# Re-planning units 0 to 3 of a hand-ordered attention and mixer kernel

## The chip, the cores and the metric

The kernel runs on one core of a Trainium2 chip. The metric is device time in microseconds (us) of one launch, here the median of several runs. The core has a matrix engine (TensorE, PE in the profile), three elementwise engines (VectorE is DVE, ScalarE is ACT, GpSimd is POOL), a queue that only issues transfers (SyncE, SP) and 16 DMA engines that the queues share. Each engine works through its own list of instructions in order; semaphores join them.

## The reference

Pooled attention, eight batches of eight heads, followed by an MLP mixer whose weights are `w_tok1`, `w_tok2`, `w_ch1` and `w_ch2`:

```python
# q, k, v: (8, 8, 576, 64); pool = 8; scale = 1 / sqrt(64)
k_p = k.reshape(B, H, Sp, pool, D).mean(axis=3)          # 72 pooled keys
v_p = v.reshape(B, H, Sp, pool, D).mean(axis=3)
scores = scale * np.matmul(q, k_p.transpose(0, 1, 3, 2))
attn = softmax(scores)                                    # written out in the original
x = np.matmul(attn, v_p) as (B, S, H * D)                 # (8, 576, 512)

h = np.maximum(x.transpose(0, 2, 1) @ w_tok1, 0.0) @ w_tok2   # 576 -> 256 -> 576
u = x + h.transpose(0, 2, 1)
h2 = np.maximum(u @ w_ch1, 0.0) @ w_ch2                       # 512 -> 1536 -> 512
return u + h2
```

## The kernel before, in words

**Units.** The last part of a batch, the channel MLP, is a *unit*: a Python generator (`unit_fast`) that issues a few matmuls and yields. Units 0 to 7 are the batches' first 512 rows, unit 8 holds the remaining 64 rows of all batches. A plain unit, which 0 to 3 are, has 45 yields, called steps 0 to 44. Steps 0 to 23 are the first layer: 12 tiles (`l1_tile`, L526) of four 128x512 matmuls, two to a step, each tile emptied from PSUM by ScalarE with a Relu into a part of `GT` (L530). Steps 24 to 44 are the second layer, made of seven products of 12 matmuls 128x256 each (L674), three steps to a product: x (24 to 26), y (27 to 29), z (30 to 32), x again (33 to 35), w (36 to 38), z again (39 to 41), x again (42 to 44). Behind each product VectorE adds the bank to what is kept so far (L717). The products are of a Strassen kind: seven stand for eight, and their operands are sums.

**Sums.** `g_sums` makes four sums of quarters of `GT`: `=3` from the first six tiles (wanted by the last x product, step 42), `=1` (by z, step 30), `=2` from `=1` (by the second x product, step 33) and `=4` from `=2` (by the second z product, step 39). `=` puts a sum on VectorE, `+` on GpSimd. `weight_sum`, written w0 to w3, makes four sums of `w_ch2` once, in unit 0, on VectorE. All work on two bf16 operands in SBUF, 128x1536. In the profile the operand tiles are called `area`, the lines are L554 and L569.

**The plan.** While a unit runs, other batches' steps are woven in. `PLAN[n]` says for unit n behind which yield which steps are issued, in the order of the text. `HEAD` is a list of the same kind for what comes before unit 0. `b.name` is a step of batch b:

- `lk`, `lv`, `lq`: loads of keys, values and queries, issued by GpSimd (L121, L131). Two buffers each (`kr`, `vr`, `qb`).
- `K0`, `K1`, `V0`, `V1`: pooling of half the heads on GpSimd (`pool8`: L177, L178 and L181 or L183); `k0`, `v1` the same on VectorE. `kpool`, `vpool0`, `vpool1`: pooling on TensorE (L256, L267).
- `kpT`: pooled keys transposed (L225), copied by ScalarE (L227). `Q0`, `Q1`: queries transposed on VectorE (L287). `s0`, `s1`, `s2`: scores (L300) and their exponentials on ScalarE (L309); s0 takes Q0, s1 takes Q1, s2 both.
- `av0` to `av4`: attention times values (L388), with the division by VectorE (L392, L331); `aw` is the same with the multiplication on ScalarE, as eight instructions (L335). Scores and these products use two large PSUM buffers in turn (`p` in the profile).
- `at0`, `at1`: the first token matmul (L400, Relu L402). `u0` to `u4`: the second (L422, L417) and the residual, added by VectorE (L423). `t0` to `t3`: u transposed by TensorE (L431) and copied by ScalarE (L432).
- `M0`, `M2`, `M4`, `M`, `MT`: u is written to memory by SyncE and read back in another order (L441, L453), and `T0` to `T5` transpose it on VectorE (L465); this takes the place of `t` from batch 3 on.
- `g`: a gate. VectorE writes one element (L840) and GpSimd copies it (L841), so what is behind it on GpSimd waits until VectorE has come there; the next gate's write waits for the copy before.

**What sets the order.** Each engine's list is the order of the text, restricted to that engine. So a step's place matters for an engine only against that engine's other instructions, and a DMA issue on GpSimd stands behind GpSimd's sums and gates. TensorE works on four small PSUM banks (`p1a` to `p1d`) which `take` and `give` hand round first in, first out: whoever takes a bank waits until the one before has been emptied.

Of the kernel before, what the change touches and what calls it, by code (L numbers as in the profile page):

```python
# [17 lines left out]
SYNC = mybir.EngineType.SP  # L18


HEAD = """LkA LkT LkB LvT Lq LvA LvB Lt1 Lk1 Lt2 Lc1b Lc1a Lq1 Lc1c Lv1 Lc1d p1 Lc2a Lc2b Lc2c d2 d2 d3 d1 d4 d4 c0 c1 prep q0 kp0 kp1 kt0 q1 d1 o0 kt1 kp2 e0 e1 q3 kt2 o1 q2 e3 vpool0 o3 e2 a00 vpool1 a02 o2 m01 d1 d1 m00 a04 X1 m03 a14 m02 X0 m04 p0 a10 a12 1.kpool m10 m14 m12 m13 m11 A1 A0 X2 X3 A2 A3"""
PLAN = [
# [13 lines left out]
def kernel(  # L36
# [829 lines left out]
    with tc.manual_schedule(engines={PE, POOLE, DVE, ACT, SYNC}):  # L866
# [8 lines left out]
        for i in range(2):  # L875
            nc.vector.memset(values[i][:, :, D], float(POOL))
            nc.vector.memset(exps[i][:, H * S:], 0.0)
            nc.vector.memset(rests[i], 0.0)
        for i, s in enumerate(HEAD.split()):
            if i == 3:  # L880
# [34 lines left out]
```

## Time and profile before

| | |
|---|---|
| median of 3 runs | 263.99 us (263.57 to 265.01) |
| time of the profiled execution | 262.58 us |
| its span, first to last instruction | 260.8 us |
| granted TensorE clock | 1.0 |
| TensorE busy | 253.0 us (97%), 2172 matmuls |
| VectorE busy | 194.9 us (75%), 391 instructions |
| GpSimd busy | 159.0 us (61%), 168 |
| ScalarE busy | 125.4 us (48%), 229 |
| GpSimd waiting at gates for VectorE | 48.4 us, 24 times |

In the profile a row of the timeline has start, duration (us), engine, line, operation, output<-inputs, shape and count, and in brackets the idle time before it with what ended it. Matmuls overlap in the pipe: one of 128x512 shows 379 ns alone and starts 0.217 us after the one before, so TensorE's pauses are read from start to start. A stage's row has, for each engine, busy time and number of instructions.

### The profile page before, as it was taken

How to read it: one execution, taken by the hardware profiler on the slowest of the kernel's cores; microseconds unless marked ns; L12 is line 12 of the kernel's file. 1: busy time of each engine (PE TensorE's matmuls, PEld its weight loads, DVE VectorE, ACT ScalarE, POOL GpSimd, SP SyncE). 2: the span in 40 equal slices, each digit the busy share in tenths (PEclk: the TensorE clock that was granted, in tenths of full speed). 3: DMA queues.
4: the chain of work that ended last, by engine and by line, in shares of the span. 5: the costliest groups of instructions: out<-in, count | busy, mean ns of one | idle time of the engine just before them, and what ended most of it. 6: DMA issues, size and time to landing. Idle time of an engine off the chain costs nothing.

```text
span 260.8 us, 5503 instructions
## 1 busy us (share of the span) xinstructions
PE 253.0 (97%) x2172; PEld 167.8 (64%) x2193; DVE 194.9 (75%) x391; ACT 125.4 (48%) x229; POOL 159.0 (61%) x168
## 2 busy tenths in 40 slices
PE   8999999999999999999999999999999999999994
PEld 3785465764666644774487447754784478888883
DVE  3557559996689756977899548954695389999993
ACT  2354876049836555565750476065525421723610
POOL 8666326899989999588939971898307912100000
PEclk9999999999999999999999999999999999999999
DMA  7999999993091989599744942840405052602304
GB/s 154 192 201 207 205 206 210 205 208 95 3 153 30 130 212 213 122 152 249 165 123 66 205 160 77 136 118 1 147 21 159 16 155 61 176 0 61 102 4 161
DMA packets 31706, 34.31 MB, mean 132 GB/s; under 512 B 3136, under 2 KB 23744, under 8 KB 31680
## 3 DMA queue, kind: packets, MB, share of 16 engines
q0 software_dynamic: 17632, 17.64, 42.5%
q1 hardware_dynamic: 13632, 15.93, 20.5%
q10 hardware_dynamic: 416, 0.39, 0.5%
q8 instruction: 17, 0.28, 0.5%
q14 instruction: 9, 0.07, 0.1%
HBM read 38.99 MB, written 12.58 MB: 198 GB/s over the span
## 4 chain that ended last, share of the span: by engine, by line
PE 89%; DVE 5%; DMA 2%; issue 2%; ACT 0%; POOL 0%; DVEq 0%; ACTq 0%; POOLq 0%
PE p1a L674 8%; PE p1c L526 8%; PE p1d L674 7%; PE p1a L526 7%; PE p1b L674 7%; PE p1b L526 7%; PE p1d L526 6%; PE p1c L674 5%; PE p L388 4%; PE p L300 3%; PE p L647 2%; DMA kr<-in_k_dram 2%; PE p1d L400 2%; PE p1b L400 2%; PE p1c L422 2%
## 5 line engine op out<-in xcount | busy, mean ns | idle before, releaser
L526 PEld LDWEIGHTS <-w_ch 128*128 128x128 bf16 x336 | 30.2, 98 | 34.0 <-issue 3.0
L674 PEld LDWEIGHTS <-area 128*128 128x128 bf16 x432 | 41.3, 98 | 7.9 <-issue 1.0
L841 POOL COPY flag<-flag 1x1 f32<-1x1 f32 x35 | 10.2, 292 | 48.5 <-DVE flag L840 48.4
L309 ACT ACTIVATE ex<-p 72x768 bf16<-72x768 f32 x42 | 31.6, 803 | 16.3 <-PE p L300 16.3
L674 PEld LDWEIGHTS <-GT 128*128 128x128 bf16 x312 | 29.6, 98 | 7.0 <-issue 1.8
L178 POOL TENSOR_TENSOR t<-t 72x512 f32<-72x512 f32 x22 | 30.6, 1389 | 1.7
L526 PE MATMUL p1c<-uT,w_ch 128*128 128x512 bf16 x89 | 24.6, 379 | 0.2
L177 POOL TENSOR_TENSOR t<-vr 72x1024 f32<-72x1024 bf16 x11 | 23.5, 2136 | 1.3 <-DMA vr<-in_v_dram 0.7
L177 POOL TENSOR_TENSOR t<-kr 72x1024 f32<-72x1024 bf16 x11 | 23.9, 2177 | 0.4
L526 PE MATMUL p1a<-uT,w_ch 128*128 128x512 bf16 x82 | 22.3, 380 | 0.2
L526 PE MATMUL p1d<-uT,w_ch 128*128 128x512 bf16 x76 | 21.6, 379 | 0.2
L526 PE MATMUL p1b<-uT,w_ch 128*128 128x512 bf16 x77 | 21.2, 379 | 0.2
L331 DVE TENSOR_TENSOR x<-p,den 128x512 bf16<-128x512 f32 x28 | 19.4, 691 | 1.0
L530 ACT ACTIVATE GT<-p1a 128x512 bf16<-128x512 f32 x21 | 12.6, 602 | 14.8 <-PE p1a L526 7.4
L530 ACT ACTIVATE GT<-p1c 128x512 bf16<-128x512 f32 x23 | 13.9, 604 | 8.3 <-PE p1c L526 8.3
L554 DVE TENSOR_TENSOR area<-GT 128x1536 bf16<-128x1536 bf16 x9 | 12.2, 1355 | 5.6 <-ACT AT L402 5.1
L530 ACT ACTIVATE GT<-p1b 128x512 bf16<-128x512 f32 x20 | 12.0, 600 | 9.1 <-PE p1b L526 5.5
L388 PEld LDWEIGHTS <-ex 72*128 72x128 bf16 x280 | 12.8, 98 | 5.3 <-DVE xt L331 0.7
L530 ACT ACTIVATE GT<-p1d 128x512 bf16<-128x512 f32 x20 | 12.0, 601 | 7.2 <-PE p1d L526 6.4
L121 POOL DMA_DIRECT2D kr<-in_k_dram x17 | 10.9, 645 | 6.5 <-PE p1c L526 2.1
L388 PE MATMUL p<-vp,ex 72*128 72x65 bf16 x280 | 14.0, 194 | 0.2 <-DVE xt L331 0.2
L423 DVE TENSOR_TENSOR u<-p1c,x 128x512 bf16<-128x512 f32 x11 | 8.0, 729 | 7.9 <-PE p1c L422 6.0
(240 smaller groups left out, 546.6 us busy)
## 6 DMA issues: line engine op xcount, KB each, us to landing
out_dram<-o SPq DMA_DIRECT2D x32, 256.0 KB, 3.8
qb<-in_q_dram POOLq DMA_DIRECT2D x7, 576.0 KB, 10.5
kr<-in_k_dram POOLq DMA_DIRECT2D x7, 512.0 KB, 9.2
vr<-in_v_dram POOLq DMA_DIRECT2D x7, 512.0 KB, 14.5
w_ch<-in_moe_w_ch_dram POOLq DMA_DIRECT2D x5, 512.0 KB, 14.7
mem<-u SPq DMA_DIRECT2D x10, 256.0 KB, 2.1
v<-mem SPq DMA_DIRECT2D x20, 128.0 KB, 2.9
area<-in_q_dram SPq DMA_DIRECT2D x2, 288.0 KB, 3.0
```

Source lines behind the costliest of these rows:

```text
L121: nc.gpsimd.dma_start(out=t[j0:j1, h0:h1].rearrange("j h i d -> j h (i d)"), in_=src[b, h0:h1].rearrange("h (j i) d -> j h (i d)", i=POOL) ...
L177: eng.tensor_tensor(out=t4[:, 0:n], in0=t[:, hs, 0:4], in1=t[:, hs, 4:8], op=ALU.add)
L178: eng.tensor_tensor(out=t4[:, 0:n, 0:2], in0=t4[:, 0:n, 0:2], in1=t4[:, 0:n, 2:4], op=ALU.add)
L309: nc.scalar.activation(out=dst, in_=src, func=AF.Exp, scale=scale)
L331: nc.vector.tensor_tensor(out=dst, in0=view, in1=den[:, :, :, None].broadcast_to([n, a, 4, D]), op=ALU.mult)
L388: nc.tensor.matmul(out=ps[:, h // 4, (h % 4) * (D + 1):(h % 4 + 1) * (D + 1)], lhsT=st["ex"][:, h * S + n0:h * S + n0 + P], rhs=st["vp"][: ...
L400: nc.tensor.matmul(out=ps, lhsT=w_tok1[:, c if c < 4 else 4 + par, m * P:(m + 1) * P], rhs=st["x"][:, c, :] if c < 4 else st["xt"], start= ...
L526: nc.tensor.matmul(out=ps, lhsT=w_ch1[:, kk, m * P:(m + 1) * P], rhs=uT[kk], start=(kk == 0), stop=(kk == 3))
L530: nc.scalar.activation(out=GT[:, :, m, :], in_=ps.rearrange("p (h n) -> p h n", h=2), func=AF.Relu)
L554: eng.tensor_tensor(out=out, in0=a, in1=b, op=ALU.subtract)
L674: nc.tensor.matmul(out=ps[i] if split else ps[:, i], lhsT=chunk(u, i, a(m)), rhs=w(m), start=start and m == 0 and (i == 0 or split), stop= ...
L841: nc.gpsimd.tensor_copy(out=flag[:, 1:2], in_=flag[:, 0:1])
```

## The change

Nothing but the two tables changes: `HEAD` gets three steps at its end that stood in unit 0, and rows 0 to 3 of `PLAN` are new. Units 4 to 8 and all functions stay. The same matmuls are issued. Besides the order:

- `3.av0` (unit 1, step 43) becomes `3.aw0`: the multiplication goes from VectorE to ScalarE.
- `=4` of unit 3 becomes `+4`: the sum goes from VectorE to GpSimd.
- Gates: unit 0 has four in place of five, at other places (17, 17, 18 and 23, the last ahead of `=1`; before 13, 18, 23, 26 and 43). Unit 1 has 3, 25, 26 and 38 (before 18, 25, 28, 38); unit 2 has 14, 20, 32, 39, 41 (before 12, 32, 38, 40); unit 3 has 34 (before 28).
- Loads: in unit 0 `2.lq` goes from step 3 to 13, `2.lv` from 8 to 19 (behind three gates), `3.lk` now comes ahead of `3.lv`. `4.lq` goes from step 11 of unit 1 to 21, `5.lk` from unit 1 to the start of unit 2, `6.lv` from the end of unit 2 to step 9 of unit 3.

```diff
--- before.py
+++ after.py
@@ -18,12 +18,12 @@
 SYNC = mybir.EngineType.SP
 
 
-HEAD = """LkA LkT LkB LvT Lq LvA LvB Lt1 Lk1 Lt2 Lc1b Lc1a Lq1 Lc1c Lv1 Lc1d p1 Lc2a Lc2b Lc2c d2 d2 d3 d1 d4 d4 c0 c1 prep q0 kp0 kp1 kt0 q1 d1 o0 kt1 kp2 e0 e1 q3 kt2 o1 q2 e3 vpool0 o3 e2 a00 vpool1 a02 o2 m01 d1 d1 m00 a04 X1 m03 a14 m02 X0 m04 p0 a10 a12 1.kpool m10 m14 m12 m13 m11 A1 A0 X2 X3 A2 A3"""
+HEAD = """LkA LkT LkB LvT Lq LvA LvB Lt1 Lk1 Lt2 Lc1b Lc1a Lq1 Lc1c Lv1 Lc1d p1 Lc2a Lc2b Lc2c d2 d2 d3 d1 d4 d4 c0 c1 prep q0 kp0 kp1 kt0 q1 d1 o0 kt1 kp2 e0 e1 q3 kt2 o1 q2 e3 vpool0 o3 e2 a00 vpool1 a02 o2 m01 d1 d1 m00 a04 X1 m03 a14 m02 X0 m04 p0 a10 a12 1.kpool m10 m14 m12 m13 m11 A1 A0 X2 X3 A2 A3 0.u1 0.u3 1.kpT"""
 PLAN = [
-    {0: "0.u0 2.lk 0.u1 1.Q0 1.Q1", 2: "1.kpT", 3: "3.lq 2.lq", 5: "0.u3", 6: "1.s0", 7: "0.u2", 8: "2.lv", 9: "1.s1", 11: "1.vpool1", 12: "1.s2 1.vpool0", 13: "=3 g", 14: "1.av2", 15: "1.av1", 17: "1.aw0", 18: "1.av4 g", 19: "w0", 20: "3.lv 1.av3", 22: "w1", 23: "g =1 =2 3.lk", 25: "1.at1 1.at0 =4", 26: "g 2.K1", 27: "2.K0", 28: "w3", 29: "2.V0", 33: "1.u0", 34: "1.u1", 35: "1.u2", 36: "w2", 37: "2.Q1 1.t2", 40: "1.u3", 41: "1.t0", 42: "1.t3", 43: "g 1.t1 3.Q0 2.Q0 1.u4"},
-    {0: "2.kpT", 1: "2.v1", 3: "2.s0", 8: "3.K1 2.s2", 9: "3.K0", 11: "4.lq", 12: "2.s1", 15: "3.Q1", 16: "2.aw3", 17: "2.av1", 18: "g", 20: "2.av0", 21: "2.av4", 23: "2.av2 =1", 24: "4.lk", 25: "g", 26: "3.kpT 2.at1", 27: "=2", 28: "2.at0 =4 g", 31: "2.u3 4.Q1", 32: "3.s2", 33: "2.t3 2.u2", 35: "3.s0 3.V1", 36: "=3", 37: "3.V0", 38: "g 2.u1", 39: "4.lv 3.s1 2.u0", 40: "5.lk", 41: "4.Q0 2.t2 2.t0", 43: "2.t1 3.av0 3.av2"},
-    {4: "4.K1", 6: "3.av3 3.av4", 9: "3.av1 4.K0", 12: "g 3.at1", 13: "6.lk", 14: "=3 3.at0", 18: "4.kpT 4.V1", 19: "3.u1 4.V0", 20: "3.u0 3.u3", 21: "3.u2 3.u4", 23: "4.s2", 24: "3.M0 3.M2", 25: "=1", 26: "3.M4", 27: "=2", 28: "4.s0", 29: "=4", 30: "3.M", 31: "4.s1 3.MT 3.T3 3.T0", 32: "g 5.lq 5.lv", 34: "3.T1", 35: "4.av4 4.aw1", 36: "3.T2", 38: "g 6.lq", 40: "g", 42: "4.aw2 6.lv"},
-    {1: "4.av0", 3: "5.K1", 5: "4.av3", 8: "4.at1", 9: "4.at0 5.k0", 10: "5.Q0", 11: "4.u2", 12: "5.V0", 13: "4.u1", 15: "5.kpT 4.u3 5.V1", 16: "4.M2", 17: "5.s0", 18: "=3 5.Q1", 19: "6.Q0", 22: "4.u0", 23: "5.s1", 24: "4.M0", 25: "3.T4 =1 3.T5", 26: "=2", 27: "=4", 28: "g", 29: "4.M", 30: "5.s2", 32: "5.av0", 35: "5.av2", 37: "5.av1", 40: "5.av3 5.av4", 42: "4.T3 4.T1 4.T0", 43: "4.T2 5.at0 5.at1"},
+    {0: "1.Q1", 1: "2.lk 0.u0", 3: "1.Q0 3.lq", 6: "1.s0 0.u2", 9: "1.s1 1.vpool0", 10: "1.vpool1", 12: "=3 1.s2", 13: "2.lq", 14: "1.av2", 15: "1.av1", 17: "g 1.av4 g", 18: "g", 19: "1.aw0 2.lv w0", 20: "3.lk 1.av3", 22: "3.lv", 23: "w1 g =1 =2 =4", 24: "1.at0", 25: "1.at1", 28: "w3", 29: "1.u1", 33: "1.u2 1.u0", 34: "2.K1", 35: "2.K0", 36: "2.V0", 37: "1.t2 w2", 39: "1.u3", 41: "1.t0", 42: "1.t3", 43: "1.t1 3.Q0 2.Q0 1.u4", 44: "2.Q1"},
+    {0: "3.K0 2.kpT", 2: "2.s0", 3: "g", 7: "2.s2", 9: "2.v1", 12: "2.s1", 16: "2.aw3", 17: "2.av1", 20: "2.av0", 21: "3.K1 2.av4 4.lq", 23: "2.av2 =3", 24: "4.lk =1", 25: "g", 26: "g =2 2.at1", 27: "3.kpT", 28: "2.at0 3.s0", 30: "2.u3 3.Q1", 31: "3.V1", 32: "2.u2", 33: "2.t3 =4", 35: "4.Q1 2.t2", 37: "3.V0", 38: "3.s2 4.lv g", 39: "2.u0", 40: "2.u1 3.s1", 41: "2.t1 2.t0", 42: "4.Q0", 43: "3.aw0 3.av2"},
+    {0: "5.lk", 1: "4.K1", 3: "3.av1", 4: "3.av4", 6: "3.av3", 9: "4.K0", 10: "6.lk", 11: "3.at0", 13: "=3", 14: "g 3.at1", 19: "3.u2 4.V0 4.kpT", 20: "3.u0 4.V1 3.u1 3.u3 g", 21: "3.M0 3.M2", 22: "3.u4", 24: "3.M4 4.s2", 27: "=1 =2", 28: "4.s0", 30: "=4 3.M", 31: "4.s1 3.MT", 32: "3.T0 3.T3 g 5.lq", 33: "5.lv", 34: "4.aw1", 35: "6.lq 4.av4", 39: "g 3.T1", 40: "3.T2", 41: "g 4.aw2"},
+    {1: "4.av0", 5: "4.av3", 9: "4.at1 4.at0 6.lv 5.k0 5.K1", 11: "4.u2 4.u1", 13: "3.T5 5.V0", 14: "5.V1 5.Q0", 15: "5.kpT 4.u3", 17: "6.Q0 5.s0 5.Q1", 19: "=3 4.M2", 22: "3.T4 4.u0", 24: "5.s1", 25: "4.M0 =1", 26: "=2", 27: "+4", 30: "5.s2", 33: "5.av2 5.av0", 34: "g", 37: "4.M 5.av1", 38: "4.T3", 39: "4.T1 5.av3", 40: "5.av4", 42: "4.T0", 43: "4.T2", 44: "5.at1 5.at0"},
     {2: "6.K1", 5: "7.lq 7.lk 5.u3", 6: "5.u2", 8: "5.u0", 10: "6.K0", 11: "6.kpT", 12: "5.u1 6.V1 6.V0", 13: "5.M0", 16: "6.s0", 17: "5.M2", 18: "5.M", 20: "7.Q1", 21: "7.Q0", 22: "6.Q1 g", 23: "=1", 24: "6.s1 =3", 26: "g", 28: "=2", 29: "6.s2 5.T1", 30: "g", 32: "g 7.lv 5.T3", 34: "5.T0 =4", 36: "g", 37: "g", 41: "5.T2", 42: "6.av3", 44: "6.av0 5.u4"},
     {0: "7.K0", 2: "6.av2", 6: "6.av1", 7: "6.av4", 8: "7.K1", 9: "6.at0 7.V1 g", 10: "7.kpT g", 12: "=3", 13: "6.at1 g", 14: "g", 17: "6.u3 7.V0", 18: "6.u1", 20: "g 6.u2 7.s0", 21: "6.u0", 24: "7.s1", 25: "=1", 27: "=2 6.M2", 32: "7.av1", 33: "6.M0 =4", 35: "6.M", 36: "7.s2", 37: "g", 39: "6.T0 6.T2", 40: "g", 41: "6.T3", 42: "6.T1", 44: "7.av2 g 7.av3"},
     {1: "Z0", 4: "7.av0", 6: "7.av4", 8: "7.at1", 10: "Z1", 15: "7.at0", 16: "Z2", 17: "7.u1 7.u0 7.M0 7.u3 7.u4", 19: "7.u2", 20: "=3 Z3", 22: "7.M2", 25: "g =1", 27: "=2 7.M", 28: "g", 33: "=4", 34: "g", 35: "g 7.T3", 37: "7.T1 7.M4 7.T2", 38: "7.T0", 42: "7.y0", 43: "g 7.y1", 44: "7.Y2"},
```

## The prediction

> **What bounds the kernel now.** I read the busy times by stage first, then TensorE's instructions in order of time, then VectorE and GpSimd side by side where TensorE paused. The stages are cut near the starts of units 0 to 4 (first L526 matmuls at 24.25, 56.68, 86.82, 114.54 and 143.97 us).
>
> ```profile
> core 0: us, PE busy (x) PEld busy (x) DVE busy (x) ACT busy (x) POOL busy (x), PEclk, DMA share, GB/s
> 26.30:56.80 30.50, 29.94 (x259) 18.97 (x261) 23.71 (x43) 16.48 (x33) 18.05 (x20) 1.00 1.21 205
> 56.80:84.50 27.70, 27.18 (x254) 16.16 (x257) 21.60 (x34) 19.04 (x37) 25.72 (x24) 1.00 0.43 83
> 84.50:113.00 28.50, 28.40 (x257) 17.61 (x257) 21.28 (x38) 15.53 (x30) 24.44 (x24) 1.00 0.78 160
> 113.00:141.00 28.00, 27.89 (x256) 17.66 (x256) 23.80 (x44) 14.98 (x33) 22.23 (x21) 1.00 0.72 157
> ```
>
> TensorE (first pair of columns) fills every stage that the change touches, at full granted clock; VectorE and GpSimd sit at 75 to 90%. A busy share is not work, so I added up start-to-start times: 0.217 us for a 128x512 matmul, 0.109 for a 128x256, 0.26 for eight of L388, 0.47 for a scores group of L300. Beyond these prices, from 24 to 144 us, TensorE loses time in four places only, three of which carry these marks:
>
> ```profile
> 40.04 0.43 PE L388 MATMUL p<-vp,ex 72*128 72x65 bf16 x8 [0.17 <-DVE xt L331]
> 50.41 1.03 PE L674 MATMUL p1c<-area,GT 128*128 128x256 bf16 x8
> 51.63 0.40 PE L431 MATMUL p1d<-ident,u 128*128 128x128 bf16 x4 [0.18 <-DVE u L423]
> 83.02 0.59 PE L422 MATMUL p1b<-AT,w_tok 128*128 128x512 bf16 x2 [0.25 <-DVE flag L840]
> ```
>
> 0.34 us before 40.04 (the pair before it began at 39.27 and needs 0.43), 0.47 between 49.86 and 51.63 (0.43 + 8 x 0.109 = 1.30 of 1.77), 0.32 before 83.02, 0.24 inside the scores group at 107.37: 1.37 us. From 144 to 230 us I find none. Each time TensorE waits for VectorE to empty a bank, or for ScalarE's exponentials.
>
> **The ceiling.** The new plan issues the same matmuls. So units 0 to 3 can give back 1.37 us at most, 0.5% of 263.99. What decides is whether the new order makes waits of its own.
>
> **Head.** 0.u1, 0.u3 and 1.kpT come 1 to 5 steps earlier. They need banks emptied by A1, A0 and A2 (VectorE's last copy 24.02 + 0.69 = 24.71; kpT arrives at 24.25 + 0.86 = 25.11). Unit 0's first tile then takes A3's bank, emptied by ScalarE at 24.45 + 0.59 = 25.04, and arrives at 25.24. VectorE does u1, u3, 1.Q1, u0, 1.Q0 by about 28.4 (three adds of 0.73, two transposes of 0.71 behind 24.71, with small gaps); 1.s0 wants 1.Q0 at about 28.7. Cost 0, with 0.1 to 0.3 us to spare; without it 0.2.
>
> **vpool0 and vpool1** move up 3 and 1 steps, to about 31.6 us. Batch 1's values land at 16.50 + 14.6 = 31.1 and 19.15 + 12.2 = 31.35. Cost 0 to 0.2; I take 0.
>
> **Loads.** On GpSimd 2.lq moves only among steps that make it wait for nothing new. 2.lv falls behind three gates, so its issue goes from 34.31 to about 40. The DMA engines are full until 58 us (205 GB/s) and loads land in the order of issue: 2.lq still lands at 49.6 and 2.lv behind it at about 52.3, as before. 3.lk and 3.lv change places, both wanted after 60 us. Cost 0.
>
> **1.aw0 behind 1.av4.** av3 (step 20) waited for av4's PSUM buffer; av4 now comes two steps earlier. The 0.34 us go: **-0.34**. The gates at 17 and 18 stand back to back: VectorE's second memset waits for GpSimd's copy of the first (0.37 between 112.79 and 113.16). This stays under VectorE's wait for the last tile's evacuation, before `=1`.
>
> **The gate before w3.** This is where I put the cost. Why these gates matter:
>
> ```profile
> 79.43 2.12 POOL L177 TENSOR_TENSOR t<-vr 72x1024 f32<-72x1024 bf16 x1
> 80.20 2.16 DVE L554 TENSOR_TENSOR area<-GT 128x1536 bf16<-128x1536 bf16 x1
> 81.63 1.87 POOL L178 TENSOR_TENSOR t<-t 72x512 f32<-72x512 f32 x1
> ```
>
> A VectorE sum over two SBUF operands takes 0.95 us alone. Begun inside a GpSimd sum, it ends 0.81 us after that one does (82.36 against 81.55), and GpSimd's next loses 0.6. The sums at 93.67 (1.96) and 126.39 (2.38) do the same. Sums that read PSUM (L717, L423) keep their times beside GpSimd. Now unit 0:
>
> ```profile
> 44.63 1.24 POOL L121 DMA_DIRECT2D kr<-in_k_dram  x2 [0.81 <-DMA kr<-in_k_dram]
> 46.30 0.95 DVE L554 TENSOR_TENSOR area<-w_ch,area 128x1536 bf16<-128x1536 bf16 x1
> 46.31 0.06 DVE L840 MEMSET flag<- 1x1 f32 x1
> 46.46 0.83 POOL L841 COPY flag<-flag 1x1 f32<-1x1 f32 x1 [0.59 <-DVE flag L840]
> 47.17 0.68 DVE L717 TENSOR_TENSOR o<-p1c,s 128x512 f32<-128x512 f32 x1
> 47.26 2.11 POOL L177 TENSOR_TENSOR t<-kr 72x1024 f32<-72x1024 bf16 x1
> ```
>
> GpSimd has its last load out at 45.87 (44.63 + 1.24; that load waited for the one eight before it, which was issued at 26.08 and landed 18.3 later). Then the gate holds it until w3 (46.30) is under way. The changed plan puts the last gate before `=1`, where VectorE passes at about 43. The last load is now 3.lv, but it too stands eight behind 2.lk, so 45.87 stays; the open gate lets 2.K1's L177 start at about 46.05. w3 still comes behind `=4` and the sum of x, at about 46.3. So w3 meets L177 and ends near 46.05 + 2.19 + 0.81 = 49.05 instead of 47.25: **VectorE is 1.8 us late**. Queued behind w3 are the sum of y, u1's add, z's sum, u2's and u0's adds. y's sum ends at 49.65. Its bank is the one that u2 takes at step 33, which TensorE reaches at about 48.5: 1.2 us lost. u0 then takes u1's bank, free at 50.35, against 50.2: 0.2. Sum **+1.4**; between 0 (w3 starts first and GpSimd waits) and 2.0 (L177 starts just ahead of w3). I take 1.4 since the row's times put L177 0.25 us ahead.
>
> **u1 to step 29, 2.Q1 to step 44, 2.K and 2.V later in the text.** VectorE's pile-up at 48 to 52 us is thinned: **-0.47** taken in either case (the 1.4 was counted from an undisturbed 48.5). The K and V sums only follow their place in GpSimd's queue, 1.2 us earlier by the paragraph above; 2.kpT (57.11, against 2.K0's end at 56.72) gains.
>
> **Unit 1.** 3.K1 is the last sum before 3.kpT: it ended at 71.39 against 71.51. It should end within 0.5 us of there (1.2 earlier, less 0.85 for w3), and 3.kpT moves one step later (0.44). `=3` leaves the collision at 80.20, `=4` moves into one; I leave the 0.32 in. 3.s1 goes from step 39 to 40: its exponentials (1.5 us from 84.3) now stand ahead of the copies of t1 and t0 on ScalarE, which end near 86.85 where unit 2 starts at 86.82: **+0.2**. 3.aw0 puts 8 x 0.22 = 1.75 us on ScalarE for 0.69 + 0.2 on VectorE; unit 2's first evacuation slips from 87.93 to about 88.6, and its bank is next wanted at 90.3. Cost 0; with the cover gone up to 0.7.
>
> **Unit 3.** `+4` on GpSimd:
>
> ```profile
> 197.13 3.08 POOL L593 TENSOR_TENSOR kr<-w_ch 128x1536 bf16<-128x1536 bf16 x1
> ```
>
> The same shape there takes 3.08 us for VectorE's 0.96. GpSimd is free from 130.70, `=2` ends at 133.75, so `+4` ends at about 137.0, and step 39 wants it at 138.59. Cost 0; a gain is excluded, as VectorE ends nothing there; with 1.6 us more on GpSimd it would cost what exceeds that. The Trainium skill (GPSIMD Engine Reference, section Performance versus the Vector engine) puts a two-input sum at 1.96 times VectorE's time, an estimate of 1.9 us here; this case's 3.08 differs and decides, and by the page the sum would be the same with 1.2 us more to spare. The skill also says (Perfetto Trace Analysis, section Optimizing Scalar/DVE Operations) that moving work between these two may not help since they share an SBUF read port; the rows at 80.20 agree on the port, and no VectorE sum over two SBUF operands lies between steps 27 and 39 to be blocked.
>
> **Sum.** -0.34 - 0.47 + 1.4 + 0.2 = +0.8 us: span 261.6, profiled time 262.58 + 0.8 = 263.4. That execution lay 1.41 under the median of the runs, so on the median's footing 263.99 + 0.8 = **264.8 us**. I count 0.5% (1.3 us) as what a measurement can tell from no change.
>
> **Rivals.** (1) *w3 is first.* If VectorE reaches w3 before about 46.05, GpSimd waits instead and the 1.4 vanishes: -0.6, **263.4**; with all four pauses gone 262.6. For it: the two starts are 0.25 us apart. Against: w3 has the same predecessors as before. (2) *VectorE stays late.* w2 (step 37) meets 2.K0's L177 early in it as well: another 1 to 2 us ahead of w's sum and u3's add, which t0's bank and t3 wait for before unit 1: +0.8 + 1.7, **266.5**. It decides if w2 comes with over 1 us of L177 left; before, at 51.48, it met a gap by luck. (3) *GpSimd is late for 3.kpT.* TensorE runs in order, so each microsecond past 72.2 costs one: with 2 us of added port waits **266.5** as well. Against: GpSimd starts 1.2 us sooner.
>
> **Chances.** Forecast 0.45 (own range 264.0 to 265.7), rival 1 0.27, rivals 2 and 3 0.28. Range **262.8 to 267.0**: down to most of rival 1, up past 266.5. Faster by over 0.5% (under 262.67) needs the whole ceiling: 0.08. Slower (over 265.31): 0.25 of the last case and a fourth of the forecast's, 0.37. Within: 0.55.
>
> **What would show it.** Right: w3 at 2.5 to 2.9 us with an L177 under it, TensorE idle over 1 us before u2 near 48.5, no wait before av3 near 40. Wrong: w3 at 0.95 and an L177 of 2.7 or more; idle before 3.kpT or unit 3's second z product. Any pause over 1 us elsewhere in units 0 to 3 overthrows the sum.

## The result, and the profile after

The changed kernel is slower: 265.15 us in the median of 22 runs (264.29 to 269.29) against 263.45 for the kernel before, in 22 runs beside it (262.34 to 265.01). The ratio is 1.0081, with a 95% interval of 1.0056 to 1.0106, so it lies above the 0.5% that the prediction counts as no change. The prediction was 264.8 us, in a range of 262.8 to 267.0, with "within 0.5%" as the likeliest case and "slower" next; the second of these came. The time is in the range and close to the middle, but the difference was forecast at 0.8 us and is 1.70 between the medians (2.06 between the two profiled executions, 264.64 and 262.58). That the level came out closer than the difference is luck: the three runs shown of before had a median 0.54 above that of the 22. The ratios leave out three runs that lie far above the others of their kernel: 269.29 us here, 669.61 in experiment 1 and 267.90 in experiment 7.

The page of the changed kernel gives its span, its busy times and the shares of the chain that ended last:

```profile
span 262.9 us, 5532 instructions
...
PE 255.2 (97%) x2193; PEld 167.9 (64%) x2193; DVE 194.5 (74%) x389; ACT 127.1 (48%) x237; POOL 159.8 (61%) x169
...
PE 83%; DVE 11%; issue 3%; ACT 1%; DVEq 0%; ACTq 0%
```

VectorE's busy time fell by 0.4 us and GpSimd's rose by 0.8. Neither says where 2 us went. The chain does better: VectorE's part of it was 5% and is 11%. TensorE's own work is the same: both profiles hold 2193 weight loads, and the profile of before has records of 2172 of its matmuls, so that the two busy times (253.0 and 255.2 us) can't be compared. The next step is to list its pauses again, start to start, as for the prediction:

| place | before, us | after, us | difference | foreseen |
|---|---|---|---|---|
| unit 0, before av3 (after: before at0) | 0.34 | 0.12 | -0.22 | -0.34 |
| unit 0, 48 to 52 us | 0.47 | 1.27 + 0.22 | +1.02 | -0.47 + 1.4 |
| unit 1, second z and u1 | 0.32 | 0.38 + 0.54 | +0.60 | 0 |
| seam of units 1 and 2 | 0 | 0 | 0 | +0.2 |
| unit 2, scores group | 0.24 | 0.23 | 0 | 0 |
| unit 4, second tile | 0 | 0.30 | +0.30 | 0 |
| unit 8, before two last products | 0.40 | 0.27 + 0.49 | +0.36 | 0 |
| sum | | | +2.06 | +0.8 |

The sum matches the 2.06 us between the profiled executions. Unit 0 lost 0.80 us net where 0.59 was foreseen; the other 1.26 stand in units 1, 4 and 8, where the prediction had 0. Unit 0 in the timeline of the changed kernel (start, duration, engine, line, operation; the bracket is the idle time before, with what ended it):

```profile
44.77 1.25 POOL L121 DMA_DIRECT2D vr<-in_v_dram  x2 [1.81 <-PE p1a L400]
...
46.16 2.11 POOL L177 TENSOR_TENSOR t<-kr 72x1024 f32<-72x1024 bf16 x1
...
46.36 2.72 DVE L554 TENSOR_TENSOR area<-w_ch,area 128x1536 bf16<-128x1536 bf16 x1
49.01 0.68 DVE L717 TENSOR_TENSOR o<-p1b,s 128x512 f32<-128x512 f32 x1
...
49.74 0.59 PE L422 MATMUL p1b<-AT,w_tok 128*128 128x512 bf16 x2 [1.11 <-DVE o L717]
50.39 0.59 PE L422 MATMUL p1c<-AT,w_tok 128*128 128x512 bf16 x2
```

The third row is w3. It was 0.95 us before; begun 0.20 behind the start of a GpSimd sum, it takes 2.72 and ends 0.81 after that sum does (49.08 against 48.27). The sum of y then empties the bank `p1b` at 49.69, and u2 starts 0.05 later. These are the predicted events, with the predicted sizes.

In unit 1 the same happens to `=4`, which now stands at step 33:

```profile
79.84 2.12 POOL L177 TENSOR_TENSOR t<-vr 72x1024 f32<-72x1024 bf16 x1
...
80.18 2.59 DVE L554 TENSOR_TENSOR area<-GT,area 128x1536 bf16<-128x1536 bf16 x1
82.69 0.68 DVE L717 TENSOR_TENSOR s<-p1c,u 128x512 f32<-128x512 f32 x1
...
82.83 0.61 PE L674 MATMUL p1a<-w_ch,area 128*128 128x256 bf16 x4 [0.32 <-DVE area L554]
...
83.98 0.65 DVE L717 TENSOR_TENSOR s<-p1b,u 128x512 f32<-128x512 f32 x1
...
84.69 0.59 PE L422 MATMUL p1b<-AT,w_tok 128*128 128x512 bf16 x2 [0.38 <-DVE flag L840]
```

The second z product wants `=4`, which ends at 82.77: first pause. VectorE is then behind with all that it has queued (a sum, a transpose, another sum), the last of which frees `p1b` at 84.63: second pause, for u1. The bracket of the last row names the gate's memset, but the bank is what came free just then.

### The profile page after: what moved, and what is told of

It is laid out like the page before. It is cut to its first block, busy times and chain, and to the rows that moved or that the text cites. A ratio compares the mean times of both kernels' runs of the same rounds, so it can differ in the third digit from the quotient of the medians.

```text
span 262.9 us, 5532 instructions
## 1 busy us (share of the span) xinstructions
PE 255.2 (97%) x2193; PEld 167.9 (64%) x2193; DVE 194.5 (74%) x389; ACT 127.1 (48%) x237; POOL 159.8 (61%) x169
## 4 chain that ended last, share of the span: by engine, by line
PE 83%; DVE 11%; issue 3%; ACT 1%; DVEq 0%; ACTq 0%
PE p1a L526 8%; PE p1a L674 7%; PE p1d L526 7%; PE p1b L526 7%; PE p1d L674 7%; PE p1c L526 6%; PE p1b L674 5%; PE p1c L674 4%; PE p L300 4%; PE p L388 3%; PE p L647 2%; DVE area L554 2%; DVE s L717 2%; PE p1c L422 2%; PE p1c L400 2%
## 5 line engine op out<-in xcount | busy, mean ns | idle before, releaser
L841 POOL COPY flag<-flag 1x1 f32<-1x1 f32 x35 | 8.3, 238 | 48.4 <-DVE flag L840 48.2
L526 PE MATMUL p1a<-uT,w_ch 128*128 128x512 bf16 x96 | 25.3, 379 | 0.1
L177 POOL TENSOR_TENSOR t<-vr 72x1024 f32<-72x1024 bf16 x11 | 23.3, 2120 | 1.1 <-DMA vr<-in_v_dram 0.5
L177 POOL TENSOR_TENSOR t<-kr 72x1024 f32<-72x1024 bf16 x11 | 23.7, 2152 | 0.4
L526 PE MATMUL p1d<-uT,w_ch 128*128 128x512 bf16 x84 | 22.9, 379 | 0.0
L526 PE MATMUL p1b<-uT,w_ch 128*128 128x512 bf16 x84 | 22.7, 379 | 0.0
L530 ACT ACTIVATE GT<-p1a 128x512 bf16<-128x512 f32 x24 | 14.4, 601 | 14.9 <-PE p1a L526 7.7
L526 PE MATMUL p1c<-uT,w_ch 128*128 128x512 bf16 x72 | 19.9, 379 | 0.0
L331 DVE TENSOR_TENSOR x<-p,den 128x512 bf16<-128x512 f32 x27 | 18.7, 692 | 0.9
L674 PE MATMUL p1a<-area,area 128*128 128x256 bf16 x132 | 16.7, 273 | 0.0
L530 ACT ACTIVATE GT<-p1c 128x512 bf16<-128x512 f32 x18 | 10.8, 601 | 7.8 <-PE p1c L526 7.7
L554 DVE TENSOR_TENSOR area<-GT 128x1536 bf16<-128x1536 bf16 x9 | 8.5, 947 | 7.6 <-ACT AT L402 5.1
```

Source lines behind the costliest of these rows:

```text
L177: eng.tensor_tensor(out=t4[:, 0:n], in0=t[:, hs, 0:4], in1=t[:, hs, 4:8], op=ALU.add)
L331: nc.vector.tensor_tensor(out=dst, in0=view, in1=den[:, :, :, None].broadcast_to([n, a, 4, D]), op=ALU.mult)
L526: nc.tensor.matmul(out=ps, lhsT=w_ch1[:, kk, m * P:(m + 1) * P], rhs=uT[kk], start=(kk == 0), stop=(kk == 3))
L530: nc.scalar.activation(out=GT[:, :, m, :], in_=ps.rearrange("p (h n) -> p h n", h=2), func=AF.Relu)
L554: eng.tensor_tensor(out=out, in0=a, in1=b, op=ALU.subtract)
L674: nc.tensor.matmul(out=ps[i] if split else ps[:, i], lhsT=chunk(u, i, a(m)), rhs=w(m), start=start and m == 0 and (i == 0 or split), stop= ...
```

## The experiments

Each ratio is against the kernel before, run beside it on the same chip, with its 95% interval. The diffs show steps of the plan, by unit.

**1. The gate of unit 0 back behind the sums.** The changed kernel, with one gate moved.

```diff
 unit 0
-23: "w1 g =1 =2 =4"
+23: "w1 =1 =2 =4", 26: "g"
```

> The changed kernel with one gate of unit 0 moved back from ahead of =1 (step 23) to step 26, ahead of w3, where the kernel before had it. Theory A (the open gate lets 2.K1's L177 start 0.2 us ahead of w3, which then waits for its end): w3 falls from 2.72 us to 0.95, the pause of 1.49 us ahead of u2 and u0 goes, and the kernel takes about 1.5 us less than the changed one, about 0.6 us more than before. Rival B (the loss comes from the later loads and from GpSimd being late as a whole): GpSimd starts 2.K1 over 1 us later than in the changed kernel, so the time rises above the changed kernel's.

Measured: 263.98 us, ratio 1.0031 (1.0017 to 1.0045). The interval doesn't touch that of the changed kernel. Its timeline:

```profile
46.75 0.95 DVE L554 TENSOR_TENSOR area<-w_ch,area 128x1536 bf16<-128x1536 bf16 x1
...
47.71 2.12 POOL L177 TENSOR_TENSOR t<-kr 72x1024 f32<-72x1024 bf16 x1
...
56.34 0.84 POOL L181 TENSOR_TENSOR kp<-t 72x256 bf16<-72x256 f32 x1
...
57.23 0.30 PE L225 MATMUL p1a<-ident,kp 72*128 72x72 bf16 x4 [0.36 <-POOL kp L181]
```

w3 is at 0.95 us again and the pauses at u2 and u0 are gone. Some of it comes back: GpSimd starts its K sums 1.55 us later, and 2.kpT now waits 0.3 us for the second of them. The gate's place is a trade of 1.49 us at u2 and u0 for 0.3 at 2.kpT, so it is worth about 1.2 us; the medians say 0.5%, 1.3 us. The waits of units 1, 4 and 8 stay.

**2. The same gate taken out of the kernel before**, and nothing else.

```diff
 unit 0
-26: "g 2.K1"
+26: "2.K1"
```

> The kernel before with its gate at step 26 of unit 0 taken out, and nothing else. Theory A: 2.K1's L177 starts near 46.1 us, w3 takes 2.6 to 2.8 us instead of 0.95, TensorE waits about 1.1 us more near u1 and u2 (steps 34 and 35), and the kernel takes 0.8 to 1.5 us more than before. Rival B: GpSimd starts 1.2 us sooner and everything behind it gains, so the time is the same or lower.

Measured: 264.99 us, ratio 1.0071 (1.0048 to 1.0095).

```profile
43.71 1.24 POOL L121 DMA_DIRECT2D kr<-in_k_dram  x2
44.97 2.13 POOL L177 TENSOR_TENSOR t<-kr 72x1024 f32<-72x1024 bf16 x1
...
44.75 3.17 DVE L554 TENSOR_TENSOR area<-GT,area 128x1536 bf16<-128x1536 bf16 x1
47.85 0.68 DVE L717 TENSOR_TENSOR s<-p1a,u 128x512 f32<-128x512 f32 x1
48.45 1.42 DVE L554 TENSOR_TENSOR area<-w_ch,area 128x1536 bf16<-128x1536 bf16 x1
...
48.58 0.60 PE L674 MATMUL p1a<-area,area 128*128 128x256 bf16 x4 [0.79 <-DVE s L717]
...
50.52 0.59 PE L422 MATMUL p1c<-AT,w_tok 128*128 128x512 bf16 x2 [0.47 <-DVE o L717]
```

One gate less in the old order costs as much as the whole change. Not all is as expected: w3 takes 1.42 us and not 2.6 to 2.8, since `=4` is hit first. GpSimd's last load did not wait here and was out at 44.95, a microsecond earlier than in the changed kernel's profile. That load waits for the landing of the one eight places before it, 2.lk, whose first part landed at 43.42 here and at 44.24 in the changed kernel's profile. So with the gate open the start of the K sums follows the landing of a load, and which of VectorE's sums are caught under them is left to that.

**3 and 4. The new head and row 0 alone, and the new rows 1 to 3 alone.**

```diff
-HEAD, PLAN[0] of before
+HEAD, PLAN[0] of the changed kernel
```

> The new HEAD and the new row of unit 0 with the old rows of units 1 to 3. Theory A: the pauses of unit 0 change from 0.81 us to 1.61, so +0.8 us against before, and nothing of the changed kernel's later pauses (82.8, 84.7, 146.6 us). Rival B (each part alone is harmless, the loss is in rows 1 to 3): within 0.3 us of before.

```diff
-PLAN[1], PLAN[2], PLAN[3] of before
+PLAN[1], PLAN[2], PLAN[3] of the changed kernel
```

> The old HEAD and row of unit 0 with the new rows of units 1 to 3. Theory A: unit 0 pauses 0.81 us as before, unit 1 pauses 0.9 us instead of 0.32 since =4 of step 33 meets GpSimd's second L177 for 3.V0, unit 4 pauses 0.3 us at its second tile; together +0.9 us against before. Rival B (the later loss is a consequence of unit 0's lateness, and goes with it): within 0.3 us of before.

Measured: 264.62 us, ratio 1.0066 (1.0036 to 1.0096), for the head and unit 0; 264.28 us, ratio 1.0045 (1.0028 to 1.0061), for units 1 to 3. Each half is slower than before by itself. The first shows the early landing too:

```profile
43.53 1.24 POOL L121 DMA_DIRECT2D vr<-in_v_dram  x2 [0.73 <-PE p1c L400]
...
44.91 2.11 POOL L177 TENSOR_TENSOR t<-kr 72x1024 f32<-72x1024 bf16 x1
...
44.74 3.10 DVE L554 TENSOR_TENSOR area<-GT,area 128x1536 bf16<-128x1536 bf16 x1
...
50.43 0.38 PE L422 MATMUL p1b<-AT,w_tok 128*128 128x512 bf16 x1 [1.34 <-DVE o L717]
...
51.88 1.91 PE L674 MATMUL p1d<-area,area 128*128 128x256 bf16 x8
```

Its page shows something else behind that pause, which starts at 48.8 and is 1.5 us long from start to start. The granted clock, in tenths for 40 slices of the span (9 is 90% or more), falls in two of them:

```profile
PEclk9999999889999999999999999999999999999999
```

Between 51.0 and 54.3 us the profile gives a granted clock of 0.50, and the matmuls 128x256 start 0.213 us apart where they start 0.109 apart before and after. Over some 3.4 us that costs about 1.7 us, an estimate from these rows. The profiles of all other kernels here keep a clock of 1.0 through unit 0.

The second has unit 0 as it was before, the pauses of unit 1 (0.36 and 0.54) and unit 4 (0.30) as in the changed kernel, and one of its own, between the old row 0 and the new row 1. 2.v1, on VectorE, was at step 1 and is at step 9, and 2.aw3 waits for it:

```profile
65.95 0.95 DVE L183 TENSOR_TENSOR vp<-t 72x256 bf16<-72x256 f32 x1
...
66.95 0.29 PE L388 MATMUL p<-vp,ex 72*128 72x65 bf16 x4 [0.89 <-DVE vp L183]
```

That pause is 1.05 us from start to start, about what the second half costs in all (1.1 us between the medians). The halves therefore don't add up to the change (0.66% and 0.45% against 0.81%), and are not to be read as its parts. What carries over are the pauses of units 1 and 4 in the second trace: they are there without the new unit 0, so they do not follow from its lateness, and the prediction put them at nothing.

**5. Unit 1's `=4` ahead of the gate**, which goes behind both sums, so that none of the GpSimd sums behind it can run under them.

```diff
 unit 1
-26: "g =2 2.at1"
+26: "=2 =4 g 2.at1"
-33: "2.t3 =4"
+33: "2.t3"
```

> The changed kernel with =4 of unit 1 moved from step 33 to step 26, behind =2 and ahead of the gate, so that it runs before GpSimd starts 3.V1. Theory A (in unit 1 the same collision costs again: =4 took 2.59 us under 3.V0's L177, and the second z product and u1 waited 0.9 us): =4 takes 0.95 us, the waits at 82.8 and 84.7 us go, and the kernel takes 0.6 to 0.9 us less than the changed one, so 0.4% instead of 0.8% over before. Rival B (GpSimd's start moves 1 us back and 3.V0 comes late for batch 3's values, or =3's old collision returns elsewhere): no gain.

Measured: 263.97 us, ratio 1.0029 (1.0008 to 1.0051), below the changed kernel's interval.

```profile
75.48 0.96 DVE L554 TENSOR_TENSOR area<-GT,area 128x1536 bf16<-128x1536 bf16 x1
...
82.44 0.61 PE L674 MATMUL p1a<-w_ch,area 128*128 128x256 bf16 x4
...
83.76 0.59 PE L422 MATMUL p1b<-AT,w_tok 128*128 128x512 bf16 x2
```

The sum is at 0.96 us, and both the z product and u1 start without a bracket. u2's pause in unit 0 stays (1.22). A little comes back here too: in unit 2 `=1`, which now comes under the end of a V sum, takes 1.32 us, and the pause there is 0.32 for 0.23.

**6. 5.at1 and 5.at0 back at step 43 of unit 3** (one run).

```diff
 unit 3
-43: "4.T2", 44: "5.at1 5.at0"
+43: "4.T2 5.at1 5.at0"
```

> The changed kernel with 5.at1 and 5.at0 moved from step 44 of unit 3 back to step 43, nothing else. Theory A (the four banks go round first in, first out: from step 44 the last x product's bank is handed on two places sooner, to unit 4's second tile, which waited 0.3 us at 146.6 us for VectorE's last sum): that wait goes and the span is 0.3 us shorter than the changed kernel's 262.9, apart from run-to-run spread. Rival B (VectorE is late at the end of unit 3 for another reason, so whichever tile comes second waits): the wait stays.

Measured: 265.58 us in one run, span 263.8. The execution was one of the early landings (L177 at 45.18, `=4` 2.90 us, w3 1.42), so its total says nothing of this edit. Locally the 0.30 before unit 4's second tile is gone, and 0.31 stands inside at1, which now comes before VectorE has its last operand ready:

```profile
144.24 0.69 DVE L331 TENSOR_TENSOR xt<-p,den 64x512 bf16<-64x512 f32 x1
...
144.99 0.38 PE L400 MATMUL p1b<-xt,w_tok 128*128 128x512 bf16 x1 [0.16 <-DVE xt L331]
```

The wait moved and did not go. The kernel before has at0 first, at the same step, and no such pause.

**7. Both moved computations back on VectorE.**

```diff
 unit 1
-43: "3.aw0 3.av2"
+43: "3.av0 3.av2"
 unit 3
-27: "+4"
+27: "=4"
```

> The changed kernel with its two moved computations taken back: unit 3's =4 on VectorE again, and 3.av0's multiplication on VectorE again. Theory A (both were hidden, cost 0): within 0.3 us of the changed kernel, 0.7 to 0.9% over before. Rival C (the slower GpSimd sum, 3.1 us against 0.95, and the 1.75 us on ScalarE against 0.69 are where the loss is): 1 us or more less than the changed kernel, within 0.3% of before.

Measured: 264.42 us, ratio 1.0051 (1.0025 to 1.0078); the interval overlaps that of the changed kernel. In the profile the pauses of units 0, 1 and 4 are as they were (1.1 before u2, 0.37, 0.54, 0.30), span 262.7 against 262.9. No pause of TensorE comes from either move. What covers `+4`, in the timeline of the changed kernel:

```profile
134.36 0.95 DVE L554 TENSOR_TENSOR area<-area,GT 128x1536 bf16<-128x1536 bf16 x1
...
135.45 3.09 POOL L554 TENSOR_TENSOR area<-GT,area 128x1536 bf16<-128x1536 bf16 x1 [3.27 <-DVE area L554]
...
140.15 0.60 PE L674 MATMUL p1d<-w_ch,area 128*128 128x256 bf16 x4
```

The first row is `=2`, the second `+4`, which ends at 138.54. The second z product, which wants it, starts at 140.15: 1.6 us to spare.

**8. The three edits of 1, 5 and 6 together.**

> The changed kernel with the gate of unit 0 back at step 26, =4 of unit 1 at step 26 and 5.at1, 5.at0 at step 43: the three places where it waits. Theory A: 1.5 + 0.7 + 0.3 us less than the changed kernel, that is 0.3 to 0.5 us less than before, less what 2.kpT waits for 2.K0 (0.3 us in the run with the gate alone): between 0.1 and 0.4 us under before. Rival B (each wait moved only exposes the next): at or over the time of the run with the gate alone, 0.3% over before.

Measured: 263.04 us, ratio 0.9992 (0.9974 to 1.0009). With three of the plan's steps put elsewhere the whole loss is gone, and the kernel is no different from the one before.

**9. The same with two more**, since 2.kpT's wait of 0.3 us was left in it.

```diff
 unit 0
-17: "g 1.av4 g", 18: "g", 19:
+17: "g 1.av4 g", 19:
 unit 1
-0: "3.K0 2.kpT", 2: "2.s0", 3: "g"
+0: "3.K0", 1: "2.kpT", 3: "2.s0 g"
```

> The changed kernel with the three repairs together (gate behind the sums ahead of w3, unit 1's =4 early, at1 and at0 at step 43), and two more: 2.kpT one step later (step 1) with 2.s0 beside the gate at step 3, and one of the two back-to-back gates of unit 0 dropped. Theory: the 0.3 us that 2.kpT waited for 2.K0 goes and nothing else changes, so 0.3 below the kernel with three repairs: ratio 0.997 to 0.999. Rival: 2.s0 one step later makes its exponentials late for 2.v1's neighbours, or the dropped gate lets a K or V sum start under a VectorE sum: ratio 1.000 to 1.003, with a VectorE sum over 1.4 us in unit 0 or 1.

Measured: 262.53 us (262.23 to 264.44), ratio 0.9977 (0.9959 to 0.9994): faster than both kernels, by 0.6 us against before. 2.kpT has no bracket any more, and w3 stays out of the K sum. What is left is, in the main, the 0.32 inside at1, the 0.40 in unit 8 that before has too, and 0.52 where unit 2's z product waits for `=1`, again under a V sum:

```profile
46.08 0.95 DVE L554 TENSOR_TENSOR area<-w_ch,area 128x1536 bf16<-128x1536 bf16 x1
...
56.87 0.29 PE L225 MATMUL p1a<-ident,kp 72*128 72x72 bf16 x4
...
104.50 1.53 DVE L569 TENSOR_TENSOR area<-GT 128x1536 bf16<-128x1536 bf16 x1
```

**10 and 11. The good parts of the change, in the kernel before.** Both edits, and the second alone.

```diff
 unit 0
-17: "1.aw0", 18: "1.av4 g"
+17: "1.av4", 18: "1.aw0 g"
 unit 1
-23: "2.av2 =1"
+23: "2.av2 =3 =1"
-36: "=3"
```

> The kernel before with only two of the changed orders: 1.av4 ahead of 1.aw0 in unit 0, and unit 1's =3 moved from step 36 to step 23, ahead of =1, out of the V sum it collided with. Theory: the pauses of 0.34 us before 40.04 and of 0.32 before 83.02 go, nothing is made: 0.66 us or 0.25% less, ratio 0.996 to 0.999. Rival: =3 at step 23 pushes the sum of unit 1's first x product 0.95 us back, the bank is late by that and the gate behind it too, so 2.at1 or z waits: ratio 0.999 to 1.003, with a new TensorE pause between 73 and 77 us.

> The kernel before with only unit 1's =3 at step 23. Theory: 0.32 us less, ratio 0.998 to 0.9995, and VectorE's =3 at 0.95 us for 2.16. Rival as for the kernel with both edits: a new pause between 73 and 77 us, ratio 0.9995 to 1.003. The difference between the two kernels is then av4's order alone: 0.34 by the theory.

Measured: 262.99 us, ratio 0.9985 (0.9969 to 1.0001), for both; 262.87 us, ratio 0.9991 (0.9976 to 1.0005), for `=3` alone. In the traces half of the theory holds: with both, the pauses before 40 us and before 83 us are gone and none stands between 73 and 77, while with `=3` alone the first (0.33) stays. `=3` took 1.20 and 0.95 us, for 2.16 before. But "nothing is made" does not hold: with both edits 3.kpT waits 0.18 us for its K sum (71.75) and a product of unit 2 starts 0.20 late (111.81), and with `=3` alone 0.32 stands before 4.kpT (125.57). The intervals hold what 0.66 and 0.32 us would give (0.9975 and 0.9988) and also 1, and the two kernels can't be told apart by time.

## Why the prediction came out as it did

**Right: the gate before w3.** Its term was +1.4 us; 1.49 was measured (1.27 + 0.22), with L177 0.20 us ahead of w3 where 0.25 had been worked out. Experiments 1 and 2 undo it in the new kernel and make it in the old one (there with `=4` caught first), so that this is the cause is shown and not only read from a trace. The Trainium skill (SBUF — State Buffer, section Who interferes with whom) says that a VectorE operation with two SBUF inputs and a GpSimd operation that reads SBUF shut each other out, and that the order in which they are issued decides which one waits. The trace agrees: w3 began 0.20 us after L177 and ended 0.81 us after it. Experiment 2 has the other order, `=4` recorded 0.22 us ahead of L177, and `=4` still took 3.17 us, which that rule alone would not give (more of this in the last section).

**Right: the first two terms.** The 0.47 of the pile-up in unit 0 went. Of the 0.34 before av3, 0.22 net went, since 0.12 turned up at at0 near 41.95.

**Mis-sized: unit 1.** "`=3` leaves the collision at 80.20, `=4` moves into one; I leave the 0.32 in." The collision was seen and its price was not worked out: two different consumers stand behind it. `=3`, hit in the kernel before, came 1.2 us late and delayed one bank by 0.32 us; it was itself not wanted before step 42, which TensorE reached 2.4 us after it was done. `=4`, hit in the new one, came 1.6 us late and is wanted at step 39, which costs 0.38, and what is queued behind it on VectorE then comes late for u1, 0.54. That is +0.60 where the sum has 0, and experiment 5 takes it away.

**Mis-sized: the seam of units 1 and 2.** The +0.2 for 3.s1's exponentials ahead of the copies did not come; TensorE has no pause where unit 2 begins.

**Not foreseen: unit 4's second tile, +0.30.** The prediction looked at the seam of units 3 and 4 only as the end of the stage. 5.at1 and 5.at0 moved one step on, behind the last x product, and so the order in which the four banks go round changed: the tile takes the bank that VectorE's last two adds of unit 3 still hold.

```profile
144.64 0.76 DVE L465 STREAM_TRANSPOSE uT<-v 128x256 uint32<-128x256 uint32 x2
...
145.32 1.25 DVE L717 TENSOR_TENSOR o<-p1a,s 128x512 f32<-128x512 f32 x2
...
146.63 1.04 PE L526 MATMUL p1a<-uT,w_ch 128*128 128x512 bf16 x4
```

VectorE has done with `p1a` at 146.57, and the matmul starts at 146.63. Experiment 6 shows that the step's place makes this wait, and that the other place has one of the same size; experiments 8 and 9 have the step there as well, no wait at the tile, and 0.33 and 0.32 us inside at1.

**Not foreseen: unit 8, +0.36**, in a unit that the change leaves alone. VectorE stands 0.46 us between two sums of which the second needs only the first:

```profile
251.51 0.95 DVE L554 TENSOR_TENSOR area<-area,GT 128x1536 bf16<-128x1536 bf16 x1
252.92 0.96 DVE L554 TENSOR_TENSOR area<-GT,area 128x1536 bf16<-128x1536 bf16 x1 [0.46 <-DVE area L554]
```

The same 0.46 us is in the profiles of experiments 1, 2, 3 and 6, and not in those of before and of experiments 4, 5 and 7 to 11, where unit 8 is the same text. Experiment 7 has unit 0's and unit 1's waits and not this one. What makes it is open.

**The rivals.** w3 did not come first, so the first rival is out. w2 did meet 2.K0's L177, with 0.69 us of it left (under the 1 us from which the second rival decides), took 1.50 us and made no pause. (In the kernel before it had met more than a gap: the L177 begun 0.24 us behind it took 2.73 us for 2.11, so there GpSimd was the one that waited.) 2.K0's sums ended at 56.22 and 2.kpT waited for nothing, nor did 3.kpT at 73.94. The second and third rivals had a further 1 to 2 us, near the 1.26 that was missing, but by waits that did not come; less than half of the 1.26, the 0.60 of unit 1, is a collision of the kind that they name. The ceiling held: the best of these orders is at 0.9977, inside the 0.5% that the pauses of before allow.

**Small slips.** GpSimd's busy share in the four stages is 59 to 93%, not 75 to 90, and the chance of "slower" adds up to 0.36, not 0.37. No forecast rests on either.

**Right: `+4` and 3.aw0 cost nothing.** All of unit 3 came some 1.5 us later than in the old trace, the end of `=2` (135.31 for 133.75) as well as the second z product (140.15 for 138.59), so the 1.6 us to spare stayed. The Trainium skill's 1.96 times VectorE's time for a two-input sum (GPSIMD Engine Reference, section Performance versus the Vector engine; measured there in fp32) is not what this sum shows: 3.09 against 0.95 us, 3.2 times.

## What to carry to other kernels

Where the sums of two engines hold each other up, price a moved operation by two things, what it will run beside and who stands behind it: 1.2 us of delay on `=3` cost TensorE 0.32 us, by a bank alone, and 1.6 us on `=4` cost it 0.92, by the operand and a bank. A gate that seems only to hold an engine back may be what keeps two instructions apart, and a load's landing decides in its place once it is gone; look at what it separates before it is moved. And when a step changes place at a seam, follow the order in which buffers go round past the end of the edited stage, since the wait can stand in the next one.

## What the runs showed that was not expected

Whether a VectorE sum that has begun is safe from GpSimd is not settled by the recorded starts. In the changed kernel one begun 0.07 us ahead of a GpSimd sum kept its time, and GpSimd's took 1.59 us for 0.85, as rival 1 of the prediction had it:

```profile
95.25 0.96 DVE L554 TENSOR_TENSOR area<-GT 128x1536 bf16<-128x1536 bf16 x1 [1.80 <-ACT GT L530]
95.32 1.59 POOL L181 TENSOR_TENSOR kp<-t 72x256 bf16<-72x256 f32 x1
```

But `=4` began 0.22 us ahead of GpSimd's sum in experiment 2 and 0.17 ahead in experiment 3, and took 3.17 and 3.10 us where it takes 0.96 alone. In these two GpSimd's sum came behind the issue of a load, in the first case behind another sum. Why the earlier start does not win in the two is open.

With the gate of unit 0 open, a run depends on when a load lands: GpSimd's K sum started at 46.16 in the changed kernel's profile and at 44.91 to 45.18 in those of experiments 2, 3 and 6, with one or two of VectorE's sums caught. In the changed kernel and experiments 3 and 6 the last load was issued 0.53 us behind the landing of 2.lk each time (44.24, 43.00 and 43.18).

The clock adds to this. Six of the changed kernel's 22 runs took 267.36 us and more and have a mean granted clock of 0.993 or 0.994; the other 16 have 0.997 to 1.0 and a median of 264.87. The same 0.994 stands at two runs each of experiments 3 and 7, the profiled one of experiment 3 among them, and at no run of the other experiments, nor of the kernel before beside them. Some 3.4 us at half clock, as in experiment 3's profile, give just this mean. If the pause sets it off, such a pause costs more than its own length, which neither the prediction nor the table of pauses counts. One trace shows the two together; that the other long runs have their half clock at the same place is likely and not shown. The length of the pause alone does not decide it, since the profile of experiment 6 has one of 1.5 us at the same place and keeps 1.0.
